# Counting tokens per expert with matmuls, and a newly found order for attention and ranking, in a fused attention, mixture-of-experts and feed-forward kernel

## The chip, the cores and the metric

The kernel runs on one core of one Trainium2 chip, in one launch. The metric is the device time of that launch in microseconds (us), lower is better. The engines are PE (TensorE), DVE (VectorE), ACT (ScalarE), POOL (GpSimd) and SP (SyncE, which here only starts transfers). Each runs its own instructions strictly in the order in which they were written and waits on semaphores for the others.

## The reference

Three layers follow one another, in float32.

```python
# attention: 4 batches, 8 heads, 768 tokens, 48 wide; the state is 48 x 48 per batch and head
k_n = k / (norm(k) + 1e-6)
for t in range(768):
    y[t] = q[t] @ state
    state = state + beta[t] * outer(k_n[t], v[t] - state.T @ k_n[t])
x = y as 3072 tokens x 384
# experts: each token goes to one of 8, weighted by its softmax probability
logits = x @ w_gate + modality_bias[modality_id]
e = argmax(logits)
x = gate * (maximum(x @ w1[e], 0) @ w2[e])        # 384 -> 1024 -> 384
# feed-forward
h = x @ w_in                                      # 384 -> 2048
out = (h * sigmoid(h)) @ w_out                    # 2048 -> 384
```

## The kernel before

**Attention.** The 768 tokens are cut into six tiles of 128 tokens (t = 0 to 5), and within a tile the 32 pairs of batch and head into two halves (p = 0, 1). In a tile the recurrence over tokens is turned into a triangular system. PE makes the products of keys and queries (`gram`, L355; DVE masks them into tiles KB, L368), ACT and DVE bring them into lanes (`to_lanes`, L394), ACT and DVE make norms and scales (L400 to L421), and then the triangular systems are solved for all pairs at once in 31 steps (`step`, L438, L456, L459). Tiles 0, 2, 3 and 5 are solved on DVE, tiles 1 and 4 on POOL. DVE spreads the solution back (`spread`, L474 for a DVE tile, L471 for a POOL tile). From there PE goes on: `join` (L487), `turn_upper` (L495), `lower` (L514), `weigh` (L530, L531), the update of the state (L547, L563) and the outputs (L577). DVE lengthens the values with the keys' norms (L426).

**Ranking.** After tile 1 and after tile 2 (and again after tiles 4 and 5) the router takes the logits (PE L879, L887, DVE L890) and ranks the tokens: `choose` (the expert as a 0/1 matrix OH, tokens x (8 or 4 groups of 128) x 8 experts), `count` (how many tokens before this one have the same expert, two matmuls L939 and L940), `place` (L948 to L959) and `gates` (the probabilities, L963 to L970). After the second call `finish` works out which tokens stand in which expert's slots: lane tables (L1044), slot bases (L1051 to L1060), selection tables (L1118) that PE collects (L1149), and the index list gidx (L1154 to L1159). With it POOL gathers the tokens of the first 1536 (`xg`, L1276), and the first experts run on PE (L1309, L1316) while the attention of tiles 3 to 5 goes on. All tokens of the second half and the feed-forward layer follow.

**What sets the order.** Attention, ranking and the first experts are one list of jobs (`plan`, L600), each with an engine, a listed duration, the jobs it needs and a rank. A list scheduler at build time (`Order.solve`) takes at each point, of the jobs of an engine that could start within 0.03 us of the earliest one, the one with the lowest rank; jobs whose results lie in PSUM also need the next of five banks, which are handed out in a ring. The order so found is the order in which each engine's instructions are written. The ranks come from a table, `PLAN["rank"]`, of some 190 numbers. Where the scheduler's own clock leaves PE idle for more than 0.35, small matmuls without use are written in (`pulse`, L750: "fillers" below), which keep PE active.

**Counting before.** `choose` ends with a running sum over the call's n groups, done on DVE: a copy, the total of the earlier calls added to the first group, log2(n) doublings of one copy and one add each (L924 to L931), the new total (L933) and a subtraction (L934). `count` then multiplies the result with a matrix of ones and adds it to the count within the group.

Of the kernel before, what the change touches and what calls it, by code (L numbers as in the profile page):

```python
# [13 lines left out]
ALU = mybir.AluOpType  # L14
AX = mybir.AxisListType
# [9 lines left out]
        kq=8.3, qb=131.9, vs=96.2, kd=87.8, gr=66.6, gq=88.5, Gc=-5.7, Kc=-272, dg=53.6, zero=-520, L=7.4, sc=-311.2,  # L25
        b2=-220.8, ln=242.1, va=527, st=306.9, sp=-210.4, ga=153.1, px=-198.7, pt=15.1, X=130.1, T=-414.2, po=6.2,
        o=566.7, w=-158.5, wc=-114, up=-190.2, uc=85.6, ps=-63.1, sc2=420.4, py=136, Y=-126, out=290, xt=-319.5,
        xc=-168.7, gt=98.5, wv1=-499.9, wv2=-51.7, wv4=29.9, wv5=319.3, one=-290, kz=153.5, ask=-786.9, gates=336.3,
        val=-545.1, fe=-181.4, xg=-820, tr=172.4, th=-22.4, tl=-196.6, s1h=544, s1l=-251.6, s2h=139.2, s2l=-109.8,
        fi=-730, rh=-194.2, rl=28.6, se=508.5, ev=-118.2, ys=-36.6, kq0=-342.1, kq1=-104.8, kq2=474.3, kq3=169.3,  # L30
        kq4=-289.9, kq5=-103, qb0=-151.9, qb1=165.5, qb2=164.7, qb3=204.9, qb4=-83, qb5=-141.1, vs0=196, vs1=-198.6,
        vs2=609.2, vs3=213.7, vs4=94.4, vs5=723.5, kd0=187.8, kd1=522.9, kd2=98.9, kd3=573.4, kd4=453.3, kd5=-80.2,
        gr0=-387.9, gr1=23.7, gr2=12.3, gr3=-35, gr4=64.9, gr5=41.1, gq0=156.1, gq1=-1.1, gq2=-137.4, gq3=-178.4,
        gq4=445.7, gq5=-83.3, Gc0=-104.8, Gc1=-13.1, Gc2=-296.6, Gc3=-153.3, Gc4=-666.7, Gc5=-500.3, Kc0=107.5,
        Kc1=109.1, Kc2=5.5, Kc3=-177.5, Kc4=71.3, Kc5=-504.4, dg0=385, dg1=-0.9, dg2=-175.4, dg3=66.7, dg4=-232.9,
        dg5=-44.5, zero0=319.8, zero1=405.3, zero2=-141.2, zero3=-156, zero4=-190.9, zero5=96, L0=-553, L1=-121.4,
        L2=96.1, L3=-53, L4=-163.6, L5=-0.7, sc0=-176.8, sc1=-208.9, sc3=-78.9, sc4=-210.6, sc5=322.6, b20=758.8,
        b21=132.4, b22=144.5, b23=-98.2, b24=35.2, b25=8.3, ln0=441.6, ln1=870.7, ln2=13.2, ln3=-179.9, ln4=129.3,
        ln5=-47.3, va0=625.9, va1=-518.8, va2=-494.7, va3=-240.9, va4=508.4, va5=123, st0=-381.7, st1=-170.6,
        st2=-64.2, st3=505.2, st4=574.5, st5=-164.6, sp0=-52.1, sp1=45.9, sp2=-0.4, sp3=-394.4, sp4=-204.6, sp5=0.5,  # L40
        ga0=-94.1, ga1=-377.3, ga2=-706, ga3=-502.8, ga4=-5.1, ga5=-194.1, px0=-469.2, px1=-283.9, px2=-39.4,
        px3=58.9, px4=357.6, px5=-168.3, pt0=-99.3, pt1=-228, pt2=-194.1, pt3=-62.3, pt4=-447.8, pt5=-127.4,
        X0=-275.3, X1=-505.8, X2=246.3, X3=612.1, X4=61.2, X5=-39.3, T0=447.9, T1=-56.2, T2=-131.4, T3=-185.4,
        T4=-490, T5=-213.9, po0=180.3, po1=-789.5, po2=-201.6, po3=20.1, po4=483, po5=32.6, o0=-768.4, o1=-367.7,
        o2=-27.1, o3=17.9, o4=-230.1, o5=20.7, w0=13.9, w1=285.4, w2=531.1, w3=-120.1, w4=5.2, w5=-165.2, wc0=-39.4,
        wc1=-525.6, wc2=-186.9, wc3=-20.6, wc4=240.7, wc5=-56.8, up0=-102.6, up1=-320.5, up2=-572.7, up3=112.7,
# [3 lines left out]
        Y2=-156.6, Y3=142.8, Y4=-45.4, Y5=-129.9, out0=-31.4, out1=335.5, out2=-77.7, out3=77.1, out4=53.1,  # L50
        out5=171.1, xt0=360.4, xt1=-697.3, xt2=29.8, xt3=-761.9, xt4=82.3, xt5=-378.8, xc0=62.7, xc1=-146.9,
        xc2=-308.8, xc3=-299, xc4=-108.6, xc5=-186.8, gt0=-119.9, gt1=249, gt2=-393.6, gt3=-396.9, gt4=-275.9,
        gt5=-409.8,
    ), half=106.1,
    ex=-155.5, n0=40, npre=36, tok=70, test=(65, 66, 67),
# [3 lines left out]
class Order:  # L59
# [16 lines left out]
    def solve(self):  # L76
# [163 lines left out]
class Attention:  # L240
# [351 lines left out]
    def plan(self, router, experts):  # L592
# [29 lines left out]
        once(("gates",), "DVE", 1.6, R.get("gates", 0), router.biases, [("ask",), ("sp", 0)])  # L622

        for t in range(T):
# [30 lines left out]
            add(("zero", t), *(("POOL", 1.0) if PLAN["lanes"][t] == "p" else ("PE", 0.5)), lambda t=t: self.clear_inverses(t),  # L655
                [("sp", old), ("clear",)])
            add(("L", t), "DVE", 1.86, lambda t=t: self.to_lanes(t),
                [("dg", t, p, e) for p in range(2) for e in range(2)] + [("st", old, 30), ("sp", t - 2)])
            add(("sc", t), "ACT", 1.6, lambda t=t: self.norms(t), [("L", t)])
            add(("b2", t), "DVE", 1.83, lambda t=t: self.scales(t), [("sc", t), ("zero", t), ("beta",)] + [("ln", t - 2, p) for p in range(2)])  # L660
            for p in range(2):
                add(("ln", t, p), "DVE", 0.88, lambda t=t, p=p: self.lengthen(t, p), [("b2", t), ("vs", t, p)])
# [6 lines left out]
            add(("sp", t), "DVE", 2.15, lambda t=t: self.spread(t), [("st", t, 30)])  # L669
            for p in range(2):  # L670
# [8 lines left out]
                add(("px", t, p), "PE", 0.92, lambda t=t, p=p: self.join(t, p), [("sp", t), ("po", t - 1, p)], bank=[("X", t, p)])  # L679
                add(("pt", t, p), "PE", 0.9, lambda t=t, p=p: self.turn_upper(t, p), [("sp", t), ("po", t - 1 + p, 1 - p)], bank=[("T", t, p)])  # L680
# [5 lines left out]
                for i in range(2):  # L686
                    add(("w", t, p, i), "PE", 0.93, lambda t=t, p=p, i=i: self.weigh(t, p, i),
                        [("o", t, p), ("kd", t, p)] + [("ga", t, p, k) for k in range(4)], bank=[("wc", t, p, i)])
                    add(("wc", t, p, i), "ACT", 1.17, lambda t=t, p=p, i=i: self.keep_weights(t, p, i), [("w", t, p, i)])
                for e in range(2):  # L690
                    prev = ("sc2", t, p, 0) if e else ("sc2", t - 1, p, 1)
                    add(("up", t, p, e), "PE", 1.02, lambda t=t, p=p, e=e: self.update(t, p, e),
# [18 lines left out]
                    add(("xt", t, p, e), "PE", 0.37, turn, [("Y", t, p, e), ("gt", t - 1, 0), ("gt", t - 1, 2)], bank=[("xc", t, p, e)])  # L711
# [3 lines left out]
            for i, (e, c) in enumerate((("PE", 0.7), ("ACT", 0.27), ("PE", 0.15), ("DVE", 0.2))):  # L715
# [45 lines left out]
class Router:  # L761
# [138 lines left out]
    def rank(self, t0, t1):  # L900
# [11 lines left out]
        def choose():  # L912
# [33 lines left out]
        def place():  # L946
# [12 lines left out]
            nc.vector.scalar_tensor_tensor(pm, pd, -128.0, r1, op0=ALU.mult, op1=ALU.add)  # L959

        def gates():
# [260 lines left out]
class Experts:  # L1222
# [124 lines left out]
    def plan(self, o):  # L1347
# [80 lines left out]
        for s in range(S + 1):  # L1428
# [9 lines left out]
            for b in blocks:  # L1438
# [8 lines left out]
                add("tl", s, 0, b, "DVE", 0.5, lambda s=s, b=b: turned(s, b, 1), [("th", s, 0, b)])  # L1447
            if s == S:
                break
            for c in range(F):  # L1450
                add("s1h", s, c, 0, "ACT", 0.5, lambda s=s, c=c: hi(s, c, 0),
                    [("fe", s, c // 2 * 2, 0)] + before("fi", s, c, 2) + (grams if (s, c) == (0, 0) else []))
                add("s1l", s, c, 0, "DVE", 0.49, lambda s=s, c=c: lo(s, c, 0), [("s1h", s, c, 0)])
# [9 lines left out]
                add("se", s, c, 0, "PE", 1.05 if three else 1.3, lambda s=s, c=c: second(s, c),  # L1463
# [505 lines left out]
```

## Time and profile before

| | us |
|---|---|
| three runs | 906.43, 904.16, 910.59 |
| median | 906.43 |
| the profiled execution, its own time | 910.43 |
| its span in the trace | 908.7 |
| PE busy | 864.3 (95% of the span) |
| DVE busy | 566.9 (62%) |
| ACT busy | 422.7 (47%) |
| POOL busy | 144.8 (16%) |

Times in the trace count from the span's start. The first 300 us hold the attention with the ranking and the first experts' work, then come the other experts and, from about 496 us, the feed-forward layer. "Busy" on PE counts the fillers as well, and counts time at the lower of PE's two clocks in full.

### The profile page before, as it was taken

The page shows a single profiled execution, that of the slowest core. Times are in us where ns is not written, and L with a number is a line of the kernel's source. Part 1 is how long each engine was busy: PE and PEld are TensorE (multiplying, and loading weights), DVE is VectorE, ACT ScalarE, POOL GpSimd, SP SyncE. Part 2 cuts the span into 40 slices and gives each one's busy share as a digit, 9 for nine tenths or more (in the row PEclk, how much of TensorE's full clock was granted, in tenths as well). Part 3 has the DMA queues.
Part 4 walks back from the last instruction along what each step waited for, and adds up shares of the span by engine and source line. Part 5 has one row for each costly group of instructions (what it writes and reads, how often), then busy time and mean ns, then how long its engine had stood idle before and what let it go on. Part 6 is the DMA issues. An engine that isn't in the chain of part 4 may idle for free. (4 is left out here: it accounts for less than half of the span.)

```text
span 908.7 us, 23189 instructions
## 1 busy us (share of the span) xinstructions
PE 864.3 (95%) x9369; PEld 743.0 (82%) x9369; DVE 566.9 (62%) x1490; ACT 422.7 (47%) x837; POOL 144.8 (16%) x211
## 2 busy tenths in 40 slices
PE   6699998899999999999997999999999999999997
PEld 5578887788887788889897888888888888888987
DVE  5999888879614988778776587442443433533332
ACT  7047666477764456555554544332333323332222
POOL 5681008700010141022110100000000000000000
PEclk9799999899999999999999999999999999999999
DMA  9937657438416236556534541130120100200200
GB/s 191 171 94 160 154 143 175 105 74 261 97 47 195 69 111 208 173 176 209 175 115 89 123 105 35 21 50 1 28 44 0 29 8 1 31 5 1 34 2 35
DMA packets 135220, 85.05 MB, mean 94 GB/s; under 512 B 102281, under 2 KB 121367, under 8 KB 135104
## 3 DMA queue, kind: packets, MB, share of 16 engines
q1 hardware_dynamic: 131904, 73.84, 33.9%
q0 software_dynamic: 3200, 9.64, 3.2%
q8 instruction: 75, 1.23, 0.6%
q14 instruction: 41, 0.34, 0.1%
HBM read 70.33 MB, written 14.35 MB: 93 GB/s over the span
## 5 line engine op out<-in xcount | busy, mean ns | idle before, releaser
L1753 PE MATMUL fpo<-fgh,o 128*128 128x512 f32 x480 | 162.0, 396 | 0.0
L1744 DVE TENSOR_TENSOR fq<-fy,fgh 128x512 fp32r<-128x512 f32 x96 | 66.1, 689 | 111.9 <-ACT fgh L1742 104.8
L1740 DVE TENSOR_TENSOR fy<-fph,fy 128x512 f32<-128x512 f32 x96 | 66.0, 689 | 97.7 <-ACT fy L1738 97.3
L1742 ACT CAST fgh<-fy 128x512 fp32r<-128x512 f32 x96 | 59.6, 621 | 134.8 <-PE fpo L1753 107.1
L1735 PE MATMUL fph<-fxh,ih 128*128 128x512 f32 x288 | 114.2, 398 | 3.2 <-ACT fxh L1717 3.2
L1735 PE MATMUL fph<-fxh,il 128*128 128x512 f32 x288 | 113.7, 395 | 0.0
L1738 ACT ACTIVATE fy<-fph 128x512 f32<-128x512 f32 x96 | 57.3, 598 | 115.7 <-PE fph L1735 109.4
L1753 PEld LDWEIGHTS fpo<-fgh,o 128*128 128x128 f32 x480 | 90.3, 188 | 21.5
L1753 PE MATMUL fpo<-fq,o 128*128 128x512 f32 x240 | 95.1, 396 | 0.0
L1316 PE MATMUL poe<-w2s,pairs 128*128 128x384 f32 x360 | 71.8, 342 | 1.6 <-ACT pairs L1488 1.6
L1316 PEld LDWEIGHTS poe<-w2s,pairs 128*128 128x128 f32 x360 | 64.3, 190 | 4.8 <-ACT pairs L1488 2.5
L1735 PEld LDWEIGHTS fph<-fxh,ih 128*128 128x128 f32 x288 | 54.7, 190 | 15.9 <-ACT fxh L1717 3.5
L1735 PEld LDWEIGHTS fph<-fxh,il 128*128 128x128 f32 x288 | 54.5, 189 | 12.4
L1309 PE MATMUL bank<-xh,wRH 128*128 128x256 f32 x240 | 55.4, 309 | 2.0 <-DVE wRH L1367 1.9
L1735 PE MATMUL fph<-fq,ih 128*128 128x512 f32 x144 | 57.1, 396 | 0.0
L1735 PE MATMUL fph<-fxl,ih 128*128 128x512 f32 x144 | 56.7, 395 | 0.0
L1753 PEld LDWEIGHTS fpo<-fq,o 128*128 128x128 f32 x240 | 45.1, 188 | 10.8
L459 DVE TENSOR_TENSOR po<-po,tmp 128x126 f32<-128x126 f32 (+35 forms) x244 | 49.9, 249 | 0.1
L456 DVE TENSOR_TENSOR tmp<-po,L 128x126 f32<-128x126 f32 (+35 forms) x244 | 49.1, 242 | 0.7
L1276 POOL DMA_INDIRECT xg<-xs,gidx x25 | 27.5, 1101 | 132.7 <-PE bank L1290 87.2
L1309 PEld LDWEIGHTS bank<-xh,wRH 128*128 128x128 f32 x240 | 39.6, 189 | 5.5 <-DVE wRH L1367 2.6
L1367 DVE TENSOR_TENSOR wRH<-raw,wRH 128x384 fp32r<-128x384 f32 x40 | 21.9, 551 | 31.4 <-ACT wRH L1364 31.3
(450 smaller groups left out, 1773.5 us busy)
## 6 DMA issues: line engine op xcount, KB each, us to landing
raw<-in_moe_w_dram SPq DMA_DIRECT2D x72, 384.0 KB
ri<-in_moe_w_in_dram SPq DMA_DIRECT2D x12, 512.0 KB
ro<-in_moe_w_out_dram SPq DMA_DIRECT2D x16, 384.0 KB
vs<-in_vd_dram SPq DMA_DIRECT2D x12, 384.0 KB
KI<-in_kd_dram SPq DMA_DIRECT2D x24, 192.0 KB
Z<-vs SPq DMA_DIRECT2D x24, 192.0 KB
xs<-Y SPq DMA_DIRECT2D x48, 96.0 KB
fy<-ys SPq DMA_DIRECT2D x72, 64.0 KB
```

The lines of the kernel that those rows point to most:

```text
L456: eng.tensor_tensor(tv, row.to_broadcast([128, n, c]), l.to_broadcast([128, n, c]), op=ALU.mult)
L459: eng.tensor_tensor(x, x, tv, op=ALU.add)
L1276: self.nc.gpsimd.indirect_dma_start(out=rows, out_offset=None, in_=self.xs[0 : self.xs.shape[0] // (2 - n), :], in_offset=bass.IndirectOff ...
L1309: self.nc.tensor.matmul(ph, a[:, k, :], b[:, k, 0:n], start=(i == 0), stop=(i == 8))
L1316: self.mark = self.nc.tensor.matmul(o, a[:, cs], b, start=(c == 0 and i == 0), stop=(c == self.F - 1 and i == 2)).ins
L1367: nc.vector.tensor_tensor(self.bufs[f"l{part + 1}"][c % 2], self.raw(part, c), self.bufs[f"h{part + 1}"][c % 2], op=ALU.subtract)
L1735: nc.tensor.matmul(ph, a[:, k, fs], b[:, k, :], start=(n == 0), stop=(n == 8))
L1738: nc.scalar.activation(sg, ph, AF.Sigmoid)
L1740: nc.vector.tensor_tensor(gv, ph, sg, op=ALU.mult)
L1742: self.marks = [nc.scalar.copy(gh, gv).ins]
L1744: self.marks.append(nc.vector.tensor_tensor(gl, gv, gh, op=ALU.subtract).ins)
L1753: nc.tensor.matmul(po[k], a[:, rows], b, start=(f == 0 and i == 0), stop=(f == 15 and i == 2))
```

## The change

Three things are edited. The running sum over the groups leaves DVE: `count` now accumulates in PSUM the matmul with the triangular matrix, from the second call on one of ones with the total, and n - 1 of ones with OH shifted by one group, two groups and so on. The total is made by DVE at the end of `place` with one reduction and one cast or add. Second, some listed durations of the plan are other numbers. Third, the table of ranks is another one (all its rows differ), the window of 0.03 us is now set for each engine, and the numbers `half` and `ex`, which shift the ranks of the later half and of the experts, are others. Lines of the changed kernel are one higher than before up to the ranking, and two lower behind it.

```diff
-        gr5=41.1, gq0=156.1, gq1=-1.1, gq2=-137.4, gq3=-178.4,
...
-    ), half=106.1,
-    ex=-155.5, n0=40, npre=36, tok=70, test=(65, 66, 67),
+        gr5=380.9, gq0=518.9, gq1=-792.8, gq2=-620.2, gq3=108, gq4=616.1, gq5=-141.6, Gc0=493.7, Gc1=-182,
...
+    ), half=211.9,
+    wait=dict(PE=0, ACT=0, DVE=0.02, POOL=0.03, SP=0.03),
+    ex=-144.9, n0=40, npre=36, tok=70, test=(65, 66, 67),
...
-                i = min((rank[i], i) for s, i in cand if s <= s0 + 0.03)[1]
+                i = min((rank[i], i) for s, i in cand if s <= s0 + PLAN["wait"][q])[1]
...
-            add(("sp", t), "DVE", 2.15, lambda t=t: self.spread(t), [("st", t, 30)])
+            add(("sp", t), "DVE", 1.87, lambda t=t: self.spread(t), [("st", t, 30)])
...
-            c = new("ca", sh, BF16)
-            nc.vector.tensor_copy(c, OH)
-            if t0:
-                nc.vector.tensor_tensor(c[:, 0], c[:, 0], total, op=ALU.add)
-            d, k = 1, 0
-            while d < n:
-                nx = new(("cb", "ca")[k % 2], sh, BF16)
-                nc.vector.tensor_copy(nx[:, :d], c[:, :d])
-                nc.vector.tensor_tensor(nx[:, d:], c[:, d:], c[:, : n - d], op=ALU.add)
-                c, d, k = nx, 2 * d, k + 1
-            nc.vector.tensor_copy(total, c[:, n - 1])
-            nc.vector.tensor_tensor(c, c, OH, op=ALU.subtract)
-            v["c"], v["df"] = c, df
+            v["df"] = df
 
         def count():
             pr = v["pr"] = sized(self.room, [128, n, E])
             nc.tensor.matmul(pr, self.tri, OH, start=True, stop=False)
-            nc.tensor.matmul(pr, self.ones, v["c"], start=False, stop=True)
+            if t0:
+                nc.tensor.matmul(pr, self.ones, total[:, None, :].to_broadcast(sh), start=False, stop=False)
+            for d in range(1, n):
+                nc.tensor.matmul(pr[:, d:], self.ones, OH[:, : n - d], start=False, stop=(d == n - 1))
...
+            here = sm.tile([128, E], F32, tag="here", name=f"here_{t0}")
+            nc.vector.tensor_reduce(here, OH.rearrange("p n e -> p e n"), axis=AX.X, op=ALU.add)
+            if t0:
+                nc.vector.tensor_tensor(total, total, here, op=ALU.add)
+            else:
+                nc.vector.tensor_copy(total, here)
```

What the new order moves is seen in the written order of an engine's instructions. On **DVE**, behind the scales of tile 3 (the two L421, L422 in the changed kernel), the kernel before has a lengthening, two key products, a tile's logits, and only then the first step of tile 3 (L438), with a pair of products between later steps:

```order
L421 TENSOR_SCALAR po_143<-b_3_2304 128x16
L421 TENSOR_SCALAR po_144<-b_3_2304 128x16
L426 TENSOR_TENSOR vs_0_1953<-vs_0_1953,nt_2300 128x768
L368 TENSOR_TENSOR KB_102<-bank_122,amask 64x512 x2
L890 TENSOR_TENSOR lg<-bank_126,tbias 128x32
L438 TENSOR_TENSOR L_2202<-L_2202,b_3_2304 128x256
L456 TENSOR_TENSOR tmp_0_0_2384<-po_143,L_2202 128x16
L456 TENSOR_TENSOR tmp_0_1_2386<-po_143,L_2202 128x15
L459 TENSOR_TENSOR po_144<-po_144,tmp_0_0_2384 128x16
L459 TENSOR_TENSOR po_143<-po_143,tmp_0_1_2386 128x15
```

Changed:

```order
L422 TENSOR_SCALAR po_143<-b_3_2286 128x16
L422 TENSOR_SCALAR po_144<-b_3_2286 128x16
L439 TENSOR_TENSOR L_2170<-L_2170,b_3_2286 128x256
L457 TENSOR_TENSOR tmp_0_0_2335<-po_143,L_2170 128x16
L457 TENSOR_TENSOR tmp_0_1_2337<-po_143,L_2170 128x15
L460 TENSOR_TENSOR po_144<-po_144,tmp_0_0_2335 128x16
L460 TENSOR_TENSOR po_143<-po_143,tmp_0_1_2337 128x15
```

The first step now stands right behind the scales; the logits and one pair of products stand ahead of the scales, and inside the steps of tile 3 there are left the turn into lanes, the scales and two products for tile 4 (before: four products more and two lengthenings). Likewise tile 0's steps hold three casts of keys where they held four products, and tile 2's steps hold nothing else.

On **PE**, the second call of `count` (ranks is the PSUM tile, tri the triangular matrix, ca the running sum from DVE) stood behind a turn of tile 3's upper half (L495):

```order
L495 MATMUL bank_124<-ident,G 64x32 x16
L939 LDWEIGHTS tri
L939 MATMUL ranks<-OH,tri 128x32
L940 LDWEIGHTS ones
L940 MATMUL ranks<-ca_3545,ones 128x32
L355 MATMUL bank_125<-KKQ_93 64x64 x16
```

Changed:

```order
L888 MATMUL bank_126<-ident,xT_0_3200 128x128
L356 MATMUL bank_123<-KKQ_93 64x64 x16
L356 MATMUL bank_124<-KKQ_93 64x64 x16
L488 MATMUL bank_125<-G 64x64 x16
L928 LDWEIGHTS tri
L928 MATMUL ranks<-OH,tri 128x32
L930 LDWEIGHTS ones
L930 MATMUL ranks<-total,ones 128x32
L932 LDWEIGHTS ones
L932 MATMUL ranks<-OH,ones 128x24
L932 LDWEIGHTS ones
L932 MATMUL ranks<-OH,ones 128x16
```

It is now five matmuls in place of two (eight in the first call), and it stands directly behind the logits (L888), two grams and a join, before any of the work of tile 3 that follows (its `lower`, turn and `weigh`).

On **POOL**, the gathers of the first experts' tokens stood behind the last step of tile 4 (A is its solution):

```order
L456 TENSOR_TENSOR tmp_29_0_3933<-A_1399,L_2682 128x60
L459 TENSOR_TENSOR A_1399<-A_1399,tmp_29_0_3933 128x2x30
L456 TENSOR_TENSOR tmp_30_0_3984<-A_1399,L_2682 128x31
L459 TENSOR_TENSOR A_1399<-A_1399,tmp_30_0_3984 128x31
L1276 DMA xg<-xs,gidx_3993 128x384 x8
```

Changed, the first two of them stand inside its steps:

```order
L439 TENSOR_TENSOR L_2792<-L_2792,b_4_2943 128x256
L457 TENSOR_TENSOR tmp_24_0_3936<-A_1314,L_2792 128x175
L460 TENSOR_TENSOR A_1314<-A_1314,tmp_24_0_3936 128x7x25
L1274 DMA xg<-xs,gidx_3933 128x384 x2
L457 TENSOR_TENSOR tmp_25_0_4036<-A_1314,L_2792 128x156
L460 TENSOR_TENSOR A_1314<-A_1314,tmp_25_0_4036 128x6x26
L457 TENSOR_TENSOR tmp_26_0_4073<-A_1314,L_2792 128x135
```

Behind the two gathers twelve instructions of tile 4's steps are left. On PE the turns of tiles 4 and 5 (L495) stand, before and after, among work that does not need them; and on SP tile 2's queries and keys are now loaded ahead of tile 1's keys.

## Rows read from the trace of the kernel before

**Rows 1.** Windows: busy us and count per engine, granted clock (1.00 full), DMA share.

```profile
120.00:180.00 60.00, 52.04 (x1451) 47.32 (x1449) 53.28 (x194) 35.68 (x76) 38.59 (x66) 0.93 0.56 142
180.00:240.00 60.00, 57.86 (x1609) 53.02 (x1610) 45.59 (x193) 44.82 (x97) 4.00 (x4) 0.99 0.54 145
```

**Rows 2.** The same windows for line 750 alone, the fillers.

```profile
120.00:180.00 60.00, 2.49 (x18) 1.52 (x18) 0.93 0.56 142
180.00:240.00 60.00, 2.21 (x14) 1.12 (x14) 0.99 0.54 145
```

**Rows 3.** Windows of the two stretches at half clock.

```profile
154.27:157.69 3.42, 3.42 (x34) 2.79 (x31) 1.62 (x7) 1.78 (x4) 3.03 (x6) 0.50 0.56 115
174.75:181.58 6.83, 6.83 (x127) 6.61 (x125) 4.45 (x16) 2.14 (x5) 3.96 (x8) 0.50 0.01 2
```

**Rows 4.** Timeline of PE: start, us, instruction, [idle before, what ended it].

```profile
153.27 0.79 PE L563 MATMUL bank<-Z,KI 128*48 128x48 f32 x26 [2.61 <-issue]
...
169.75 0.31 PE L530 MATMUL bank<-KA,KI 64*48 64x64 f32 x2 [2.14 <-DVE lg L890]
...
174.18 0.18 PE L940 MATMUL ranks<-ca,ones 128*128 128x32 bf16 x1 [1.20 <-DVE ca L934]
```

**Rows 5.** Waits of PE, 120 to 240 us: total, times, longest.

```profile
PE bank L563 <- issue: 4.7, 6, 2.6
```

**Rows 6.** Timeline of DVE: products, first step and spread of tile 3.

```profile
114.14 1.39 DVE L368 TENSOR_TENSOR KB<-bank,amask 64x512 f32<-64x512 f32 x2 [1.33 <-PE bank L355]
...
117.31 0.41 DVE L438 TENSOR_TENSOR L<-L,b 128x256 f32<-128x256 f32 x1
...
119.63 1.38 DVE L368 TENSOR_TENSOR KB<-bank,amask 64x512 f32<-64x512 f32 x2
...
131.19 2.77 DVE L368 TENSOR_TENSOR KB<-bank,amask 64x512 f32<-64x512 f32 x4
...
150.42 1.91 DVE L474 STREAM_TRANSPOSE G<-po 128x512 f32<-128x512 f32 x2
```

**Rows 7.** Timeline of DVE: logits, first and last of both running sums, lane tables.

```profile
155.94 0.19 DVE L890 TENSOR_TENSOR lg<-bank,tbias 128x32 f32<-128x32 f32 x1 [2.81 <-PE bank L887]
...
158.12 0.73 DVE L924 COPY ca<-OH 128x64 bf16<-128x64 bf16 x1
...
161.72 0.19 DVE L934 TENSOR_TENSOR cb<-cb,OH 128x64 bf16<-128x64 bf16 x1
...
171.93 0.17 DVE L924 COPY ca<-OH 128x32 bf16<-128x32 bf16 x1
...
173.85 0.27 DVE L934 TENSOR_TENSOR ca<-ca,OH 128x32 bf16<-128x32 bf16 x1
...
175.70 1.89 DVE L1044 TENSOR_TENSOR Af<-lane,pm 128x1536 bf16<-128x1536 f32 x1
```

**Rows 8.** Timeline of DVE: index list, tile 5's scales and first step, spreads.

```profile
190.06 0.17 DVE L1159 CAST gidx<-giff 128x10 int32<-128x10 f32 x1
...
190.76 1.93 DVE L471 STREAM_TRANSPOSE G<-A 128x1024 f32<-128x1024 f32 x1
...
201.69 0.41 DVE L438 TENSOR_TENSOR L<-L,b 128x256 f32<-128x256 f32 x1
...
231.03 2.00 DVE L474 STREAM_TRANSPOSE G<-po 128x512 f32<-128x512 f32 x2
```

**Rows 9.** Timeline of POOL: late steps of tile 4, first gather.

```profile
172.56 0.45 POOL L456 TENSOR_TENSOR tmp<-A,L 128x156 f32<-128x156 f32 x1
...
176.05 1.74 POOL L459 TENSOR_TENSOR A<-A,tmp 128x87 f32<-128x87 f32 x1
...
179.01 0.25 POOL L459 TENSOR_TENSOR A<-A,tmp 128x31 f32<-128x31 f32 x1
190.52 1.16 POOL L1276 DMA_INDIRECT xg<-xs,gidx  x1 [11.27 <-DVE gidx L1159]
```

**Rows 10.** Windows for line 1149 alone: 48 and 24 small matmuls, packed.

```profile
312.00:323.60 11.60, 2.97 (x48) 2.80 (x48) 1.00 0.05 18
188.80:194.70 5.90, 0.92 (x24) 0.81 (x24) 1.00 0.39 99
```

More of the change, by code (lines that the diff above doesn't have):

```diff
@@ L24 @@
     rank=dict(
[L25 to L34, printed above, removed]
@@ L50 @@
[L50 to L53, printed above, removed]
-    ), half=106.1,
-    ex=-155.5, n0=40, npre=36, tok=70, test=(65, 66, 67),
+        kq=-346.4, qb=137.4, vs=-297.6, kd=516.1, gr=-418.2, gq=432, Gc=-688, Kc=-306.4, dg=-1037.3, zero=-428.1,
@@ new lines @@
+        L=-120.2, sc=-218.1, b2=-653.7, ln=551, va=-347.9, st=469.4, sp=-470.3, ga=-322.2, px=46.2, pt=-487.2,
+        X=-97.1, T=324.2, po=226.9, o=-259, w=39.2, wc=189.8, up=-532.9, uc=58.9, ps=-264.1, sc2=-2.4, py=134.6,
+        Y=135, out=-155.4, xt=-414.5, xc=45.3, gt=-318.9, wv1=-721.3, wv2=-129.5, wv4=54.8, wv5=-192.8, one=152.4,
+        kz=1.1, ask=-589.3, gates=431.9, val=-691.9, fe=24.6, xg=-710.7, tr=-46.6, th=342.3, tl=-987.3, s1h=-683.8,
+        s1l=-420.7, s2h=256.6, s2l=-163.5, fi=271.8, rh=373.9, rl=465.3, se=-117.4, ev=-305.9, ys=450.6, kq0=-431.5,
@@ L621, in plan @@
             once(("cc", j), "DVE", 0.25, 0, cast, [("ci", j)])
-        once(("gates",), "DVE", 1.6, R.get("gates", 0), router.biases, [("ask",), ("sp", 0)])
+        once(("gates",), "DVE", 1.95, R.get("gates", 0), router.biases, [("ask",), ("sp", 0)])
         for t in range(T):
@@ L654, in plan @@
             old = self.same(t)
-            add(("zero", t), *(("POOL", 1.0) if PLAN["lanes"][t] == "p" else ("PE", 0.5)), lambda t=t: self.clear_inverses(t),
+            add(("zero", t), *(("POOL", 1.0) if PLAN["lanes"][t] == "p" else ("PE", 0.8)), lambda t=t: self.clear_inverses(t),
                 [("sp", old), ("clear",)])
-            add(("L", t), "DVE", 1.86, lambda t=t: self.to_lanes(t),
+            add(("L", t), "DVE", 1.92, lambda t=t: self.to_lanes(t),
                 [("dg", t, p, e) for p in range(2) for e in range(2)] + [("st", old, 30), ("sp", t - 2)])
             add(("sc", t), "ACT", 1.6, lambda t=t: self.norms(t), [("L", t)])
-            add(("b2", t), "DVE", 1.83, lambda t=t: self.scales(t), [("sc", t), ("zero", t), ("beta",)] + [("ln", t - 2, p) for p in range(2)])
+            add(("b2", t), "DVE", 1.92, lambda t=t: self.scales(t), [("sc", t), ("zero", t), ("beta",)] + [("ln", t - 2, p) for p in range(2)])
             for p in range(2):
-                add(("ln", t, p), "DVE", 0.88, lambda t=t, p=p: self.lengthen(t, p), [("b2", t), ("vs", t, p)])
+                add(("ln", t, p), "DVE", 0.94, lambda t=t, p=p: self.lengthen(t, p), [("b2", t), ("vs", t, p)])
                 for e in range(2):
@@ L714, in plan @@
             g = router.gate(t)
-            for i, (e, c) in enumerate((("PE", 0.7), ("ACT", 0.27), ("PE", 0.15), ("DVE", 0.2))):
+            for i, (e, c) in enumerate((("PE", 0.88), ("ACT", 0.27), ("PE", 0.3), ("DVE", 0.2))):
                 add(("gt", t, i), e, c, lambda g=g: next(g, None),
@@ L972, in rank @@
         return [
-            ("choose", "DVE", 2.6, choose, ()), ("count", "PE", 0.1, count, ("choose",)),
-            ("exps", "ACT", 1.55, exps, ("choose",)), ("place", "DVE", 1.3, place, ("count",)),
-            ("gates", "DVE", 1.6, gates, ("exps",)),
+            ("choose", "DVE", (1.2, 1.7)[n > B], choose, ()), ("count", "PE", 0.35, count, ("choose",)),
+            ("exps", "ACT", 1.55, exps, ("choose",)), ("place", "DVE", (1.6, 2.6)[t1 <= self.T // 2], place, ("count",)),
+            ("gates", "DVE", 1.65, gates, ("exps",)),
         ]
@@ L1446, in plan @@
                 add("th", s, 0, b, "ACT", 0.45, lambda s=s, b=b: turned(s, b, 0), [("tr", s, 0, b)] + old.get(s, [("fi", s - 2, F - 1, 0)]))
-                add("tl", s, 0, b, "DVE", 0.5, lambda s=s, b=b: turned(s, b, 1), [("th", s, 0, b)])
+                add("tl", s, 0, b, "DVE", 0.48, lambda s=s, b=b: turned(s, b, 1), [("th", s, 0, b)])
             if s == S:
@@ L1462, in plan @@
                     add("s2l", s, c, 0, "DVE", 0.5, lambda s=s, c=c: lo(s, c, 1), [("s2h", s, c, 0)])
-                add("se", s, c, 0, "PE", 1.05 if three else 1.3, lambda s=s, c=c: second(s, c),
+                add("se", s, c, 0, "PE", 1.07 if three else 1.35, lambda s=s, c=c: second(s, c),
                     [("rh", s, c, 0), ("fe", s, c // 2 * 2, 1)] + [("rl", s, c, 0), ("s2l", s, c, 0)] * three + before("se", s, c, 1)
```

51 lines of the change are left out of this document (29 added, 22 removed).

## The prediction

> **What bounds the kernel now.** I first read the busy times by windows of 60 us, to see which engine is short of work and where. Between 120 and 240 us PE is busy for 52.0 and 57.9 us of 120 [rows 1]: it is nearly always at work, so only what PE loses there can be won, and 120 - 52.04 - 57.86 = 10.1 us are idle. Then the same windows for the fillers alone: 2.49 + 2.21 = 4.7 us of the busy time is work without use [rows 2]. Then the granted clock: in two stretches, 3.4 and 6.8 us long, it is 0.50, the lower of the two levels, 1.2 GHz, and PE is busy all through them [rows 3]; at the full clock the same work takes half as long, so (3.42 + 6.83) / 2 = 5.1 us are lost there. Both stretches follow waits: 2.61 us at 153.27, and 2.14 and 1.20 us at 169.75 and 174.18 [rows 4]. Together 10.1 + 4.7 + 5.1 = 19.9 us is what a better order of attention and ranking could win at most in this part; the experts and the feed-forward layer that follow are the same work, and PE is their bound too.
>
> Next I asked whom PE waits for. One kind of wait has no other engine behind it: 4.7 us before L563 end with "issue", one of them 2.6 us long [rows 5]. An order cannot do much about those. The others end with DVE: with a tile's logits (2.14 us) and with the last instruction of the running sum (1.20 us) [rows 4]. So DVE is late, and its timeline says why: tile 3's steps start at 117.31 and their result is spread at 150.42, 33.1 us, with products for other tiles between the steps [rows 6]; then come logits, ranking and the index list, which is ready at 190.06; tile 5's steps start at 201.69 only, and its spread is at 231.03 [rows 7, 8]. POOL is done with tile 4 at 179.3 and idle for 11.27 us until the first gather [rows 9], so it has room.
>
> **The change, part by part.**
>
> *Running sum off DVE.* In the first call it reaches from 158.12 to 161.91, in the second from 171.93 to 174.12 [rows 7]: 3.8 + 2.2 = 6.0 us on the way to the index list. What comes in its place on DVE is one reduction and one cast or add a call. The nearest rows are small operations of 0.17 to 0.73 us [rows 7]; by 0.3 each that is 0.6 a call, 1.2 in all, and -4.8 us on DVE. Bounds: 0.7 and 2.9, so -5.3 to -3.1.
>
> *Matmuls added.* Four calls with 8, 5, 9 and 5 matmuls in place of two each: 19 more, nine of them before 240 us. Small packed matmuls take 2.97/48 = 0.06 and 0.92/24 = 0.04 us each [rows 10], a single one 0.18 from start to end [rows 4]. They follow each other without a wait, so I take 0.06 and +1.2 us on PE, which has no cover for it; bounds 0.04 x 19 = +0.7 and 0.18 x 19 = +3.4.
>
> *DVE's order.* Tile 0's steps hold three casts in place of four products (2.77 us for four [rows 6]), and tile 2's nothing, so I expect tile 1's and 2's spreads about 3 us earlier. Before about 120 us I give this nothing on PE: the banks that the early grams fill are freed by the same products, which are only moved behind tile 0's spread; bounds 0 and -2. In tile 3 the first step follows its scales at once; two waits for PE's banks, 1.33 us at the products among them [rows 6], are moved ahead of the scales, and I get 0.6 more. Inside the steps go one pair of products, 1.38, half of the four, 1.39 [rows 6], and two lengthenings and a short wait, together some 2.7: -5.5. Tile 3's spread comes so at 150.4 - 3 - 0.6 - 5.5 = 141.3, 9 us earlier.
>
> *Ranking.* Before, from that spread to the index list it is 190.06 - 150.42 = 39.6 us [rows 6, 8]. From this go 4.8 (running sum) and 1.6 (the second call's gates, now behind the index list); 2.8 come in (two pairs of products ahead of it). So 36.0, and the list at about 177 instead of 190; bounds 175 and 181, by the wait for the logits, 2.81 us before [rows 7], staying or growing.
>
> *Gathers into tile 4's steps.* Two gathers at 1.16 us [rows 9] now stand before the last twelve instructions of tile 4, which took from 172.56 to 179.26, 6.7 us [rows 9]. Everything behind them waits for the list: with the list at g, tile 4 ends at g + 0.3 + 2.3 + 6.7 = g + 9.3, its spread and one pair of products take 1.9 and 1.4 [rows 6, 8], and tile 5's steps, which DVE has behind them, start at g + 12.6. For g = 177 this is 190, 12 us earlier than 201.69; so is tile 5's spread, at 219 instead of 231. Break-even is g = 201.7 - 12.6 = 189.
>
> A row speaks against this part: beside DVE's lane tables (175.70, 1.89 us long [rows 7]) one step of POOL took 1.74 us, where the shorter last one took 0.25 [rows 9]; and copies of DVE that took 0.73 in the first running sum took 0.17 in the second, later in tile 4 [rows 7]. So the two engines hold each other up. The Trainium skill, "SBUF — State Buffer", section "Who interferes with whom", has a rule for it: a DVE operation with two inputs in SBUF, or in a 2-port mode, and a GpSimd operation that reads SBUF exclude each other for the whole instruction. The long step agrees with the rule, the short copies of the second call only in part. By the rule, with tile 4's end now beside the index work, the list and the tile would both come later than my walk has them; by the rows alone I add 1 us to each, which stays within the bounds. The case where it becomes large is a rival below.
>
> *New waits of PE.* PE's own order is strict, so work on tile 3 that comes earlier only helps if nothing in front of it waits. The second count stands behind two grams and a join, about 3 us of work, while DVE needs from the logits to the last of OH some 2.2 us plus the products in front; I estimate a wait of 2.8 us there, with the first tile-3 work queued behind it, and 2.5 us at the turn of tile 5, which needs the spread at 219. Bounds: 0, and 4 each. After waits of 2 us and more the clock fell twice [rows 3, 4], so I add one stretch like the shorter, 3.42/2 = 1.7 us.
>
> *Loads on SP and listed durations.* Tile 2's queries and keys are loaded ahead of tile 1's keys. Tile 1 is solved on POOL in the cover of tile 0's and 2's steps, so I cost this at nothing; without that cover it is at most the time of the load moved ahead, some 2 us at the start. The listed durations, `wait`, `half` and `ex` execute nothing; they count through the order alone.
>
> **The sum.** Of 19.9 us there stay: issue waits 2.1 + 2.6/2 = 3.4 [rows 5] and half of the remaining 1.5 us of short waits, 4.1 together; new waits 5.3; half clock 1.7; fillers 0.5; that is 11.6. Won are 8.3, less 1.2 for the matmuls, so -7.1 us, and with some 0.7 from the part before 120 us -7.8. Against the profiled execution's own 910.4 us this is 902.6. That execution is 4.0 us above the median of the three runs, 906.43; against the median it gives 898.6, so **899 us**.
>
> **The rivals.**
>
> *All of it is won.* If PE has so much tile-3 work before each new wait that count and turn are ready in time, no wait of 2 us is left, and the clock stays up: 19.9 - 1.4 (short waits) - 1.2 = 17.3, 906.4 - 17.3 = **889 us**. For it speaks that the list, tile 4 and tile 5 all come 9 to 13 us earlier; against it that waits for issue, of (4.7 - 2.6)/5 = 0.4 us on average but for the longest [rows 5], have no engine behind them that an order could move.
>
> *The waits only change their place.* PE waits 4 us at each of the two points, the clock falls after each for as long as before (5.1 us), issue waits stay whole (4.7 + 0.8): 8 + 5.1 + 5.5 + 0.5 + 1.2 = 20.3 against 19.9, **907 us**. For it: three stretches of DVE's chain end at such points, and five banks in a ring leave PE little other work.
>
> *Slower, by the gathers in tile 4.* The list is on DVE's chain, which runs beside POOL's steps, and tile 4 now waits for it, while before POOL had 11 us to spare. If some 35 small operations of ranking and slots take 0.6 each, as beside POOL in the first call [rows 7], in place of 0.17, this is 35 x 0.43 = 15 us: the list comes at 192, beyond the break-even of 189. With POOL's own twelve instructions held up by 6 us more, tile 5 starts at 192 + 12.6 + 6 = 210.6, 9 us late, PE runs out of attention work, and with a clock stretch more it is about **917 us**. Against it: the subtraction at the end of that same first call took 0.19 us beside POOL's steps [rows 7].
>
> *The order does nothing*, since PE is nearly full in both: 906.4 + 1.2 for the matmuls = 908 us, and this shares the third case's chance.
>
> **How the numbers follow.** First case 0.48 (its own range 892 to 904), all won 0.17, waits moved or nothing 0.25, slower 0.10. The likeliest gives 899. The range from **887 to 908** leaves out the fourth case and the tails of the others. About 1%, 9.1 us, is what a measurement of this kernel tells from no change: below 897.4 lie the second case and somewhat over half of the first, **faster 0.45**; between lie the rest of the first and most of the third, **same 0.43**; **slower 0.12** is the fourth and a little of the third.
>
> **What would show it.** In the profile after: tile 3's spread near 141, the index list near 177, tile 4's spread near 188 and tile 5's near 219; the granted clock between 120 and 240 us at 1.00 but for one stretch; fillers there under 1 us; waits of PE at the count and at L496 of 2 to 3 us each. The prediction is wrong if POOL's gathers wait long with tile 4 behind them, or if PE's idle time between 120 and 240 us stays near 10 us with the waits at other lines.

## The result, and the profile after

The changed kernel takes 914.25 us (median of 20 runs, 907.27 to 921.26), the kernel before 907.21 (20 runs): **ratio 1.0073, 95% interval 1.0053 to 1.0092**. It is slower by 0.7%, where 899 us, between 887 and 908, and a gain were forecast. A second set of 12 runs gave 912.16 us and 1.0072 (1.0047 to 1.0098). The profiled execution took 913.85 us, span 912.1. The profiled execution of the kernel before took 910.43 us, 3.2 above its median: differences between the two traces show where time went, and their sum is 3.4 us, not the 7.0 of the medians.

What was to be won on PE between 120 and 240 us was won, and more, though not by the marks that were forecast for DVE. Windows of the changed kernel, columns as in [rows 1], the second pair for the fillers' line alone:

```profile
120.00:180.00 60.00, 57.25 (x1783) 53.36 (x1779) 56.14 (x212) 45.27 (x98) 27.93 (x43) 1.00 0.70 163
180.00:240.00 60.00, 56.08 (x1488) 50.31 (x1489) 49.51 (x197) 42.26 (x91) 15.61 (x28) 1.00 0.55 145
```

```profile
120.00:180.00 60.00, 0.00 (x0) 0.00 (x0) 1.00 0.70 163
180.00:240.00 60.00, 0.78 (x4) 0.23 (x4) 1.00 0.55 145
```

Idle time fell from 10.1 to 6.7 us, fillers from 4.7 to 0.8, and no stretch of half clock is left against [rows 3]. The loss is earlier. The window behind tile 0's spread, first of the kernel before, then of the changed one:

```profile
52.00:72.00 20.00, 18.91 (x588) 17.79 (x588) 18.65 (x36) 12.69 (x27) 17.00 (x34) 1.00 0.42 96
```

```profile
52.00:72.00 20.00, 17.66 (x303) 14.66 (x304) 15.99 (x26) 3.04 (x6) 16.70 (x32) 0.66 0.22 48
```

PE runs 303 matmuls there instead of 588, at a mean clock of 0.66. Its timeline shows the beginning (start, us, instruction, [idle before, what ended it]), and a window the stretch at the lower clock:

```profile
54.36 1.12 PE L496 MATMUL bank<-ident,G 32*64 32x32 f32 x32 [2.34 <-DVE KB L369]
...
55.80 1.97 PE L356 MATMUL bank<-KB,KKQ 48*64 48x64 f32 x32
```

```profile
55.60:69.30 13.70, 13.70 (x196) 11.15 (x196) 10.36 (x17) 2.52 (x5) 12.13 (x22) 0.50 0.24 58
```

PE waits 2.34 us for DVE's product, which empties a bank. Behind it a gram takes 1.97 us; the first of the same form after the stretch takes 1.15:

```profile
70.03 1.15 PE L356 MATMUL bank<-KB,KKQ 48*64 48x64 f32 x32
```

DVE's timeline says why the bank is late, and what follows:

```profile
47.91 1.93 DVE L475 STREAM_TRANSPOSE G<-po 128x512 f32<-128x512 f32 x2
49.88 2.94 DVE L479 COPY KA<-G 32x512 f32<-32x512 f32 x4
52.82 1.39 DVE L369 TENSOR_TENSOR KB<-bank,amask 64x512 f32<-64x512 f32 x2
...
69.83 1.39 DVE L369 TENSOR_TENSOR KB<-bank,amask 64x512 f32<-64x512 f32 x2 [3.53 <-PE bank L356]
...
82.67 1.97 DVE L395 STREAM_TRANSPOSE L<-G 128x1024 f32<-128x1024 f32 x1 [1.30 <-DMA Z<-vs]
...
109.04 1.97 DVE L475 STREAM_TRANSPOSE G<-po 128x512 f32<-128x512 f32 x2
```

The products that no longer stand inside tile 0's steps come behind the spread and four casts. Until 52.82 all five banks hold grams that wait for them. With PE at half clock, DVE waits for PE in turn (3.53 us), tile 2's turn into lanes comes at 82.67, and its spread at 109.04. In the kernel before:

```profile
71.81 1.96 DVE L394 STREAM_TRANSPOSE L<-G 128x1024 f32<-128x1024 f32 x1
...
103.94 1.96 DVE L474 STREAM_TRANSPOSE G<-po 128x512 f32<-128x512 f32 x2
```

Not all of these 5 us are the banks'. In this execution tile 1's turn into lanes, which stands inside tile 0's steps, waited 3.09 us; in a second profile of the changed kernel (the run "again" below) it did not, and tile 2's spread came at 105.44. First the changed kernel, then the second profile:

```profile
24.41 1.93 DVE L395 STREAM_TRANSPOSE L<-G 128x1024 f32<-128x1024 f32 x1 [3.09 <-ACT G L375]
```

```profile
21.21 1.90 DVE L395 STREAM_TRANSPOSE L<-G 128x1024 f32<-128x1024 f32 x1
...
105.44 2.00 DVE L475 STREAM_TRANSPOSE G<-po 128x512 f32<-128x512 f32 x2
```

PE was at half clock from 14.7 to 28.3 us in the first and from 21.2 to 28.0 in the second, which is the likely reason, not a shown one. The later marks of the changed kernel, which answer to [rows 6 to 8]:

```profile
151.63 1.95 DVE L475 STREAM_TRANSPOSE G<-po 128x512 f32<-128x512 f32 x2
...
189.16 0.17 DVE L1157 CAST gidx<-giff 128x10 int32<-128x10 f32 x1
...
201.32 1.97 DVE L472 STREAM_TRANSPOSE G<-A 128x1024 f32<-128x1024 f32 x1
...
204.75 0.43 DVE L439 TENSOR_TENSOR L<-L,b 128x256 f32<-128x256 f32 x1
...
230.86 1.96 DVE L475 STREAM_TRANSPOSE G<-po 128x512 f32<-128x512 f32 x2
```

So in this execution the faster DVE of the middle only made up for the 5 us by which tile 2 was late.

**An account of PE's time.** From PE's records I added up, for each profiled execution, the time with no record (idle), the time covered by fillers alone, and half of the time that other records cover while the clock is 0.50. What is left of the span is PE's work as it would take at full clock. Halving takes off somewhat too much (the gram above takes 1.97 us at half clock and 1.15 at full, 1.7 times), so a profile with much half clock shows somewhat too little work: of the new order's profiles below, the two with the most of it, the changed kernel's and e5's, show the least.

| profile | span | idle, fillers, half clock | work |
|---|---|---|---|
| before | 908.7 | 76.2 | 832.5 |
| e4, old order, new counting | 901.0 | 68.4 | 832.6 |
| changed | 912.1 | 75.9 | 836.2 |
| changed, again | 908.5 | 71.3 | 837.2 |
| e1, e2, e3 | 907.0, 909.5, 905.0 | 70.1, 72.4, 68.3 | 836.9, 837.1, 836.7 |
| e5, new order, old counting | 918.7 | 82.3 | 836.4 |
| e6 | 900.9 | 63.6 | 837.3 |
| e8 | 901.8 | 70.8 | 831.0 |
| e9 | 898.8 | 69.7 | 829.1 |

The middle column varies by several us from execution to execution; the work is the same within 1.1 us in all seven profiles with the new order and nothing moved on PE, and 3.7 to 4.8 us above the old order's. That is a second loss beside the first 72 us. It lies in attention, ranking and the first experts: from the point on where both written orders are the same to the end (362.9 and 359.6 us) the work is 535.2 us in both. By stretches, changed minus before: 52 to 72 us +8.5, 72 to 120 us +2.0, 120 to 240 us -11.5, 240 to 300 us +1.7, the rest of the span -1.1, and work +3.7.

These are single executions. Up to 72 us the middle column holds 37.4 us before, 45.9 changed, but 42.3 in the second profile of the changed kernel and 42.4 in e5, which has its order: most of the difference is the late start of this execution, whose turn begins at 54.36 where the second profile's begins at 51.10. Between 120 and 240 us it holds 18.7 before and 7.2 changed in both profiles, but 13.1 in e4, which has the old order: against that execution the gain is 5.9, not 11.5.

### The profile page after: what moved, and what is told of

Same layout as the page of the kernel before. It is cut to its first block, busy times and chain, and to the rows that moved or that the text cites. A ratio compares the mean times of both kernels' runs of the same rounds, so it can differ in the third digit from the quotient of the medians.

```text
span 912.1 us, 23159 instructions
## 1 busy us (share of the span) xinstructions
PE 874.1 (96%) x9358; PEld 747.8 (82%) x9358; DVE 561.2 (62%) x1463; ACT 425.1 (47%) x837; POOL 146.3 (16%) x211
## 5 line engine op out<-in xcount | busy, mean ns | idle before, releaser
L1307 PE MATMUL bank<-xh,wRH 128*128 128x256 f32 x240 | 51.1, 295 | 0.5 <-DVE wRH L1365 0.5
L369 DVE TENSOR_TENSOR KB<-bank,amask 64x512 f32<-64x512 f32 x48 | 33.0, 687 | 14.9 <-PE bank L356 14.2
```

The source lines that it names most:

```text
L369: nc.vector.tensor_tensor(KB[rs, e, 8 * i : 8 * i + 8, :], gr[rs], self.amask[rs, None, :].to_broadcast([64, 8, 64]), op=ALU.mult)
L1307: self.nc.tensor.matmul(ph, a[:, k, :], b[:, k, 0:n], start=(i == 0), stop=(i == 8))
```

## The experiments

Times are medians of 6 to 12 runs beside 20 to 35 runs of the kernel before; ratios are against it, and can differ from the quotient of the two medians by up to 0.2%. In e1, e2, e6, e8 and e9 the order found is edited by a list of moves, each of which puts a job right behind another. A job is named by its kind, tile, half and part: Kc is a pair of products, st a step, ga a cast, gq a gram, px a join, po a lower. Lines of the edited kernels stand further down by the length of the list. The part that moves the jobs:

```diff
+        for key, behind in MOVES:
+            j, x = jobs[ids[key]], jobs[ids[behind]]
+            self.line.remove(j)
+            self.line.insert(self.line.index(x) + 1, j)
+            j["start"] = x["start"]
         return self.line
```

**e1: products back.**

```diff
+MOVES = [
+    (('Kc', 0, 0, 0), ('st', 0, 9)),
+    (('Kc', 0, 0, 1), ('Kc', 0, 0, 0)),
+]
```

> The changed kernel with one thing undone: the first two product jobs (four instructions of about 0.7 us, which empty two of PE's five banks) are back inside tile 0's steps on DVE, behind step 9. Theory A (the banks): with products left until after tile 0's spread all five banks are full when PE wants the turn of tile 0 at 52 us; PE waits 2.34 us, its clock falls to half for some 14 us, and about 7 us are lost that never come back in full. Then the wait is gone here, the granted clock between 52 and 72 us is 1.00, and the time falls by 5 to 8 us, to about the kernel before (ratio 0.998 to 1.003), although the spread of tile 0 is 2.8 us later. Theory B (the order itself): join and turn of tile 0 stand behind more grams and DVE has ten products in a row, so tile 0's chain is late whatever the clock; then the time stays within 2 us of the changed kernel (ratio 1.005 to 1.010).

908.9 us, ratio 1.0052 (1.0028 to 1.0077). The wait and the low clock are gone, as theory A has it:

```profile
52.00:72.00 20.00, 19.35 (x526) 17.03 (x525) 18.34 (x27) 9.20 (x19) 17.55 (x31) 1.00 0.28 67
```

But the ratio lies in theory B's range, under the changed kernel's, and the intervals overlap; the two medians alone (908.9 and 906.23) give 1.0029. Two stretches of half clock of 3.4 us come up later, at 77.5 and 132.1.

**e2: casts late.**

```diff
+MOVES = [
+    (('ga', 0, 0, 1), ('Kc', 1, 0, 1)),
+    (('ga', 0, 0, 3), ('ga', 0, 0, 1)),
+    (('ga', 0, 1, 1), ('ga', 0, 0, 3)),
+    (('ga', 0, 1, 3), ('ga', 0, 1, 1)),
+]
```

> The changed kernel with DVE's four casts of tile 0's solution (2.94 us, directly behind its spread) moved behind the first four product jobs; nothing moves on PE. Theory A: the first bank comes free some 1.4 us after the spread instead of 4.4, before PE's fillers end, so the wait of 2.34 us goes, the clock stays up, and the time falls by 5 to 8 us to a ratio of 0.998 to 1.003 against the kernel before. Theory B: no change against the changed kernel, 1.005 to 1.010, since the join still stands behind the grams.

908.45 us, ratio 1.0014 (0.9983 to 1.0045), in theory A's range. The wait at the turn is gone, but another of 2.16 us comes up some 8 us later, at a gram that needs the next bank, and with it a stretch of half clock of 6.8 us (58.7 to 65.5) in place of 13.7:

```profile
59.21 3.68 PE L369 MATMUL bank<-KRH 48*64 48x64 f32 x64 [2.16 <-DVE KB L382]
```

**e3: fillers.**

```diff
+                if j["key"] == ("pt", 0, 0):
+                    for _ in range(12):
+                        pulse()
                 j["fn"]()
```

> The changed kernel with 24 more fillers on PE directly ahead of tile 0's first turn; no order is changed, DVE is as before. They fill the wait of 2.34 us with work without use. If the wait itself is the price, nothing is won (2 us at most). Theory A in its narrow form (the price is the fallen clock, 14 us at half, not the wait): the clock stays at 1.00 from 52 to 72 us, and the time falls by 4 to 7 us, ratio 0.999 to 1.004. Theory B: 1.005 to 1.010.

910.2 us, ratio 1.0057 (1.0035 to 1.0079). With the wait filled by work without use the clock between 52 and 72 us is 1.00, as in e1 and e6, where the pause is gone by other means. So here the low clock came with the pause. In this execution it fell 20 us later instead, behind a wait of 1.33 us:

```profile
75.30 1.73 PE L491 MATMUL bank<-G 32*64 32x64 f32 x32 [1.33 <-ACT Xt L510]
```

```profile
75.60:85.90 10.30, 10.30 (x191) 9.74 (x187) 8.32 (x44) 3.80 (x8) 0.38 (x2) 0.50 0.87 164
```

What is won at one place is partly lost at another, and the ratio lies in theory B's range and cannot be told from the changed kernel's.

**e4: the counting alone**, in the old order.

> The kernel before with the counting of the change alone (old ranks, old listed durations, so the old order; the one or two more DVE instructions stand at the end of place). By theory A the loss lies in the order of the first 70 us and the counting is harmless: PE's waits for the running sum (0.63 and 1.20 us) go, 9 matmuls more before 240 us cost some 0.5, the list of tokens comes 4 to 5 us earlier, and the time is 0 to 3 us below the kernel before (ratio 0.997 to 1.000). A rival C (the added matmuls and their loads of weights cost PE more than DVE wins) gives 1.002 to 1.004.

909.2 us, ratio 1.0024 (0.9997 to 1.0050): not the gain expected, and no clear loss, though the ratio itself lies in rival C's range. Work is 832.6 us, so by the account the matmuls cost 0.1 to 0.2 us, not 1.2, and rival C's reason is not seen. The list comes at 183.7 instead of 190.1, but this order makes nothing of it:

```profile
148.63 1.91 DVE L474 STREAM_TRANSPOSE G<-po 128x512 f32<-128x512 f32 x2
...
183.69 0.17 DVE L1156 CAST gidx<-giff 128x10 int32<-128x10 f32 x1
```

**The changed kernel again.** 

> The changed kernel unchanged, timed beside the others on one chip. Ratio 1.005 to 1.009. Its PE lost 76 us to idle time, fillers and half clock in the first profile, as the kernel before (76), and did 836 us of other work at full clock where the kernel before did 832.5. If this second number is a property of the order and not of the run, it is 836 +- 0.5 here too, wherever the clock falls; if it is noise of the record, it comes out anywhere between 832 and 838.

912.16 us, ratio 1.0072 (1.0047 to 1.0098). The wait and the half clock are in this profile too, and the work is 837.2, 0.7 above the range expected:

```profile
51.10 1.25 PE L496 MATMUL bank<-ident,G 32*64 32x32 f32 x32 [2.34 <-DVE KB L369]
```

```profile
51.90:65.60 13.70, 13.70 (x193) 10.87 (x191) 10.77 (x17) 2.59 (x5) 12.13 (x22) 0.50 0.16 47
```

Without the late start of the first profile DVE's marks are 3.6 to 4.5 us earlier, and this execution still took 910.22 us, beside a median of 906.25 of the kernel before:

```profile
147.80 1.99 DVE L475 STREAM_TRANSPOSE G<-po 128x512 f32<-128x512 f32 x2
...
184.69 0.17 DVE L1157 CAST gidx<-giff 128x10 int32<-128x10 f32 x1
...
201.06 0.42 DVE L439 TENSOR_TENSOR L<-L,b 128x256 f32<-128x256 f32 x1
...
227.28 1.97 DVE L475 STREAM_TRANSPOSE G<-po 128x512 f32<-128x512 f32 x2
```

**e5: the new order with the old counting.** 

> The changed kernel's order and listed durations with the old running sum on DVE (two count matmuls a call, nine or ten more DVE instructions in choose, none at the end of place). Theory A: the loss is the order's, so this is as slow as the changed kernel or 1 to 3 us slower, ratio 1.006 to 1.012, with the token list 4 to 6 us later (194 us). Rival C (the counting costs PE): faster than the changed kernel, 1.001 to 1.004.

918.72 us, ratio 1.0123 (1.0079 to 1.0166), the list at 195.7: 6.6 us above the changed kernel beside it, more than expected. The new order needs the new counting: PE's waits between 120 and 240 us (total, times, longest) now have the running sum at their head,

```profile
PE ranks L941 <- DVE cb L935: 2.6, 1, 2.6
PE ranks L941 <- DVE ca L935: 1.9, 1, 1.9
```

where the changed kernel waits 0.27 us for a count. Rival C falls: with the old counting the new order is slower, not faster.

**e6: e1 and e2 together.** 

> The changed kernel with both edits on DVE: the first two product jobs back in tile 0's steps and the four casts behind the second two. Each alone won 5 to 6 us in the median. Theory A (it is PE's banks and the clock behind them): both together give no more than the better one, since one free bank is enough, ratio 1.000 to 1.003; PE idle time plus half clock between 52 and 120 us stays under 5 us (changed kernel 12.0). If the wait behind the fourth gram after the spread (2.16 us with the casts late) is what is left, it goes too and the ratio is 0.996 to 0.999.

909.49 us, ratio 1.0024 (0.9995 to 1.0053), no better than e2. The mean of its 12 runs is 4.8 us below that of the 12 runs of the changed kernel beside it (95% interval 2.2 to 7.4): about so much of the loss are the banks and what follows from them. In the profiled execution, the fastest of its runs (902.63 us), the clock is at 1.00 from 43 to 487 us and DVE meets its marks:

```profile
141.71 1.08 DVE L491 STREAM_TRANSPOSE G<-po 128x512 f32<-128x512 f32 x1
...
178.02 0.17 DVE L1173 CAST gidx<-giff 128x10 int32<-128x10 f32 x1
...
219.35 1.08 DVE L491 STREAM_TRANSPOSE G<-po 128x512 f32<-128x512 f32 x1
```

141.3, 177 and 219 were forecast. With the banks free, the walk through DVE's order was right, and the kernel is still not faster than the one before: its work is 837.3.

**e7: e6 with jobs moved on PE.** 

> As e6_both_early, and on PE seven jobs are moved next to one of their own kind (both joins of tile 0 behind its first turn, the second join of tile 1 behind the first, three weigh or query-gram jobs and two grams of tile 3 likewise). Theory D (PE's extra work): where PE goes from one kind of job to another without overlap, the first matmul of the new job takes 0.17 to 0.20 us instead of 0.03 to 0.05; the new order has 113 such starts between 50 and 300 us where the old one has 94, and 19 x 0.18 = 3.4 us is the extra work. Then here some 8 to 12 starts fewer, and PE's work at full clock 1.5 to 2 us lower than in e6_both_early (about 835 instead of 837), the ratio 0.001 to 0.003 lower. If the starts are no cause, the work stays at 837.

920.65 us. Eight jobs were moved, not seven. Through the moves five jobs get banks whose former content is not yet read, so a part of attention's products is of other data, and with them the tokens of each expert; the time says nothing of theory D. Its work is 836.1 us, between the 835 of theory D and the 837 of no effect. By the written order it has 135 changes, 10 fewer than e6; but it has much more half clock (by the account 17.2 us lost against 3.1), which makes the work look smaller, so that it settles nothing. The next two move jobs only where the banks' readers stand ahead.

**e8: fewer changes of the array.** Sixteen jobs, such as

```diff
+    (('po', 0, 0), ('gq', 2, 1, 1)),
...
+    (('px', 1, 1), ('px', 1, 0)),
...
+    (('gq', 4, 1, 1), ('gq', 4, 1, 0)),
```

> As e6_both_early (the changed kernel with two products back in tile 0's steps and the casts late), and sixteen of PE's jobs are moved ahead by up to five jobs, to stand beside a job whose matmuls use the same part of the array (32, 64 or 128 rows; 64 or 128 columns). By the written order PE changes between such kinds 122 times instead of 145 from the first to the last job of attention; the kernel before has 125, and 122 to 125 is what its counting and order give. Theory D: every change costs 0.15 to 0.2 us that the records show as busy (the first matmul behind it adds 0.17 to 0.20 us instead of 0.03 to 0.05). Then PE's work at full clock without fillers is 3.5 to 4.5 us lower than in e6_both_early, 833 instead of 837, and the ratio 0.996 to 0.999. Rival E (the extra work has another cause, for example the experts' matmuls standing differently between the attention's): work stays at 836.5 to 837.5 and the ratio at 1.001 to 1.004.

Work 831.0 us, 6.3 less than e6: theory D, and more than expected. One place shows it. PE in e6, a gram, a join, a lower, a turn and the next gram (48 and 64 rows, 32 rows, 64, 32, 48):

```profile
61.52 1.15 PE L372 MATMUL bank<-KB,KKQ 48*64 48x64 f32 x32
62.59 1.15 PE L504 MATMUL bank<-G 32*64 32x64 f32 x32
63.67 1.15 PE L531 MATMUL bank<-Xx,Xt 64*64 64x64 f32 x32
64.75 1.12 PE L512 MATMUL bank<-ident,G 32*64 32x32 f32 x32
65.80 0.39 PE L372 MATMUL bank<-KKQ 48*64 48x64 f32 x6
```

and in e8 with the lower moved next to the gram (each view ends at 66 us, inside the last gram):

```profile
61.49 0.97 PE L388 MATMUL bank<-KB,KKQ 48*64 48x64 f32 x26
...
62.43 0.98 PE L547 MATMUL bank<-Xx,Xt 64*64 64x64 f32 x27
63.33 0.97 PE L520 MATMUL bank<-G 32*64 32x64 f32 x26
...
64.29 0.93 PE L528 MATMUL bank<-ident,G 32*64 32x32 f32 x26
65.14 1.03 PE L388 MATMUL bank<-KKQ 48*64 48x64 f32 x28
```

The four jobs take 65.80 - 61.52 = 4.28 us in e6 and 65.14 - 61.49 = 3.65 in e8: two changes of kind instead of four. Where two neighbours use the array alike, their matmuls run into one another (the rows left out alternate between the two). Yet the time is 906.4 us beside 903.48 of the kernel before, and the ratio 1.0045 (1.0020 to 1.0069), a miss: idle time from 120 to 180 us grew from 2.9 to 6.3 us and three stretches of half clock came back (75.8 to 79.2, 171.4 to 178.2, 198.7 to 202.1).

**e9: the same on the old order with the new counting**, eight jobs.

> The kernel before with the counting alone (e4_count_only, ratio 1.0024, work 832.6 us) and eight of PE's jobs moved likewise: 111 changes instead of 125. Theory D: work 2 to 2.8 us lower, about 830, and the ratio 0.998 to 1.001. Rival E: work 832.5 and 1.001 to 1.004. A wait of a moved job for its input can take back up to 1 us of this.

**898.85 us beside 903.48 of the kernel before, ratio 0.9947 (0.9923 to 0.9970)**: faster than it by 0.5%. Work is 829.1, 3.5 us below e4, again more than expected. The rest of the gain against e4's ratio is within the two intervals.

## Why the prediction was wrong, by its steps

- **The step that failed first** is "before about 120 us I give this nothing on PE: the banks that the early grams fill are freed by the same products, which are only moved behind tile 0's spread", with bounds of 0 and -2. Only moved was the point: until they run, PE has no bank, and DVE has a spread and four casts ahead of them. Up to 72 us this cost 8.5 us in the changed kernel's profile and 4.9 and 5.0 in the two others with its order (again, e5); the first is worse mainly by its late start. e1, e3 and e6 show that the pause brings the half clock there, in the three profiles of the new order without such an edit for 13.7 us each. In the runs, e2 wins some 0.6%, e1 and e3 0.2% within overlapping intervals, and e6, with the banks free, 4.8 us. The sum, for its part, took 0.7 us of gain from this stretch, for which the working has nothing.
- **A term was missing.** The sum took PE's other work as the same in both orders, but for 1.2 us of matmuls. It is 3.7 to 4.8 us more, in every profile. The written order of PE's jobs changes between 32, 64 and 128 rows (or 32, 64 and 128 columns) 145 times, the old one 125 times; by e6 to e8 a change costs 6.3/23 = 0.27 us, by e4 to e9 3.5/14 = 0.25, which makes 20 x 0.25 = 5 us. This price is a quotient of two works, with its bias by half clock in it, not a measured interval. That the work falls with the changes is shown twice (e8, e9); that the time falls with it, by e9 alone, while e8's did not. The Trainium skill, "TensorEngine Tiling (Array Packing)", section "Key Properties", states that changing the tiling mode drains the engine. The runs agree and give the price; this rule spoke against the change, and I had not weighed it.
- **Between 120 and 240 us** the sum was right in kind: 11.5 us won where 8.3 were forecast, and 5.9 against e4's execution. How near the size came is in part luck, since the forecast rests on one execution of the kernel before that had lost 5.1 us to the clock there. The new waits of 5.3 us did not come (0.27 at the second count, none at tile 5's turn), and not in e6 either, where DVE is on time (0.6 at the count); the clock stretch of 1.7 is missing in the first profile and there in the second (178.2 to 181.6).
- **DVE's walk** missed its marks by 10 to 13 us (151.63, 189.16, 230.86), and by 6.5 to 8.3 us in the second profile. Most of it is tile 2's late spread, forecast near 101; e6, with that spread at 101.29, meets the marks within about 1 us.
- **Running sum and matmuls.** In e4 the list comes 6.4 us earlier. From tile 3's spread it is 35.1 us (148.63 to 183.69) in place of 39.6, 4.6 us less, and 4.8 were forecast: this term was right. The added matmuls were put at +1.2 us and cost 0.1 to 0.2 by the account.
- **The gathers**, the rival on the slower side, did little: here the list came at 189.16, near the break-even of 189, POOL waited 1.70 us for it, and tile 4 ended at 197.34, 8.2 us behind the list (9.3 forecast). Tile 5's first step came at 204.75, 3 us late: 15.6 us behind the list, not 12.6, so that the break-even was too late by as much. In the second profile the list comes at 184.69 and the first step at 201.06, before the old 201.69, and that execution, too, was slower than the median of the kernel before. Slower it was, but by another mechanism, which none of the rivals held.

Open stays why e8's lower work is lost again in waits while e9's is kept, and with it how much of the loss of 0.7% is the extra work: the banks make 4.8 us of it, give or take 2.6, and the loss of clock differs by several us between executions.

## What to carry to other kernels

Moving work off the busy engine's way is not free if that work empties a buffer that the engine needs: ask what each queue holds until then. Count what an order does to the bottleneck engine itself, here the changes between matmuls of 32, 64 and 128 rows; a scheduler that lists one duration for a job does not see them. And compare profiles by an account (idle, fillers, half clock, work), because the total hides the gain of the middle behind two losses; and profile each order more than once, since one execution can be 3 us late by itself.

## What the runs showed of the hardware

A change of the array's use costs about 0.25 us, estimated from the works of e6 and e8 and of e4 and e9, and the records show it as busy time, not as a wait: jobs of 32 matmuls between others of another kind take 1.05 to 1.08 us from start to start in e6's rows, neighbours of like kind 0.85 to 0.96 in e8's. PE stayed at half clock for 13.7 us while its records left no gap, behind a wait of 2.34 us, and in e3 for 10.3 us, behind one of 1.33. The same gram took 1.7 times as long there, 1.97 us against 1.15.
